# Block-wise attention with a gated feed-forward layer: the transposes of q and k moved from the tensor engine to the DMA crossbar

## The chip, the cores and the metric

The kernel runs on one core of one Trainium2 chip. The metric is the time of one execution on the device in microseconds (us). The engines are named as in the profile: PE (matmul; PEld is its weight load, which overlaps), DVE (VectorE), ACT (ScalarE), POOL (GpSimd), SP (SyncE). Here POOL issues all loads but one small one, and SP issues all stores and, after the change, the crossbar transposes. Sixteen DMA engines serve both queues.

## The reference

```python
q, k, v: [4, 8, 768, 64] float32;  lam: [8]
for each block of the sequence:                     # a decayed linear attention
    out   = (q_b k_b^T * D) v_b + (q_b * lam_pow) kv_state
    kv_state = lam_block * kv_state + (k_b * rev_pow)^T v_b
x   = out as [3072, 512]
res = (sigmoid(x @ w_gate) * (x @ w_val)) @ w_out   # 512 -> 1536 -> 512
```

The recurrence can be cut into blocks of any length. The kernel takes blocks of 128 positions: six blocks, n = 0 to 5, each with all 4 batches and 8 heads.

## The kernel before

q, k and v arrive with positions on the partitions. The scores need q and k with the head dimension on the partitions, so both are transposed. Before the change PE does it: 16 transposes of q and k for each pair of batches ("piece t"), then DVE multiplies q by its decay (QS), and ACT copies k out of PSUM (KS).

```python
qkv = ctx.enter_context(tc.tile_pool(name="qkv", bufs=NSTEP))      # six blocks resident
ps_at ... bufs=5 (PSUM);  ps_ff ... bufs=3 (PSUM)

def piece_t(n, bp):                                  # bp: pair of batches
    tq, tk = two PSUM tiles [128, 2, HP, C] bf16
    ... 8 x nc.tensor.transpose(tq[...], Q[n][...], ident)
    QS[n, bp] = trsb.tile([128, 2, HP, C], BF16, tag="QS", name="QS")
    nc.vector.tensor_tensor(out=QS[n, bp], in0=tq, in1=lamq..., op=ALU.mult)
    ... 8 x nc.tensor.transpose(tk[...], K[n][...], ident)
    KS[n, bp] = trsb.tile([128, 2, HP, C], BF16, tag="KS", name="KS")
    nc.scalar.copy(KS[n, bp], tk)

def piece_s(n, bs): ...   # scores sp <- KS, QS on PE;  piece_m: MT <- sp * mask on DVE
def piece_a(n, bs): ...   # op <- QS, Sb (state) and MT, V on PE; XT <- op on ACT
def make_kd(n): ...       # kd <- K[n] * decay on POOL, for the state update piece_c
def piece_gv(n, ft): ...  # gp = WG x, vp = WV x (4 matmuls each), sg = sigmoid(gp) on ACT,
                          # ht = sg * vp on DVE: one "gate/value unit"; 12 of them a block
def piece_po(n, tt): ...  # po = ht WO (12 matmuls), ob on ACT, store on SP; 4 a block

# the order in which POOL issues loads around block 1:
make_kd(0)
load(1, "qk", 0, 2); load_gv(5, DFF // 6); load(1, "qk", 2, 4)   # halves: batches 0-1, 2-3
load(1, "v", 0, 2);  load(1, "v", 2, 4)
for i in range(3): load_wo(i, NFT // 3)                          # output weights WO
make_kd(1)
...
for i, u in enumerate(units):      # units: gate/value and output units of all blocks in order
    if i in loads:                 # i = start of block n-1
        n = loads[i]
        load(n, "qkv", 0, B)
        make_kd(n)
    u()
    for p in after[i]: p()         # attention pieces of the next block, between the units
```

The attention of block n is spread between the feed-forward units of block n-1. The program's order is fixed on each engine; an engine that waits holds back all that stands behind it.

Of the kernel before, what the change touches and what calls it, by code (L numbers as in the profile page):

```python
# [9 lines left out]
BF16 = mybir.dt.bfloat16  # L10
AF = mybir.ActivationFunctionType
ALU = mybir.AluOpType
# [4 lines left out]
def kernel(  # L17
# [11 lines left out]
    nc = tc.nc  # L29

    B, H, S, D = q.shape
    C = 128
    NSTEP = S // C
    HP = H // 2
# [5 lines left out]
    NB2 = B // 2  # L40

    const = ctx.enter_context(tc.tile_pool(name="const", bufs=1))
    qkv = ctx.enter_context(tc.tile_pool(name="qkv", bufs=NSTEP))
    kdp = ctx.enter_context(tc.tile_pool(name="kdp", bufs=2))
    trsb = ctx.enter_context(tc.tile_pool(name="trsb", bufs=3))
    mtp = ctx.enter_context(tc.tile_pool(name="mtp", bufs=4))
# [19 lines left out]
    wv_r = moe_w_val.rearrange("(mt p) f -> p mt f", p=128)  # L66
    wo_r = moe_w_out.rearrange("(ft p) m -> p ft m", p=128)

    Q, K, V = [], [], []

    for n in range(NSTEP):
        for t, lst in (("qb", Q), ("kb", K), ("vb", V)):
            lst.append(qkv.tile([128, B, H, D], BF16, tag=t, name=t))

    def load(n, what, b0, b1):
        sl = slice(n * C, (n + 1) * C)
        for c in what:
            t, src = {"q": (Q[n], q), "k": (K[n], k), "v": (V[n], v)}[c]
            nc.gpsimd.dma_start(  # L79
                out=t[:, b0:b1],  # L80
                in_=src[b0:b1, :, sl, :].rearrange("b h s d -> s (b h) d"))
# [15 lines left out]
    tri = const.tile([128, C], FP32, tag="tri")  # L97

    load(0, "q", 0, 2)
    for i, base in enumerate((-1, C - 1)):  # L100
        nc.gpsimd.iota(jn[:, i:i + 1], pattern=[[0, 1]], base=base, channel_multiplier=-1,
                       allow_small_or_imprecise_dtypes=True)
    load(0, "k", 0, 2)
    make_upper_triangular(nc, tri, val=1.0, diag=True)
    load(0, "q", 2, 4)
    nc.gpsimd.iota(ip1, pattern=[[1, C]], base=1, channel_multiplier=0,
                   allow_small_or_imprecise_dtypes=True)
# [16 lines left out]
    lamq = const.tile([128, HP, C], BF16, tag="lamq")  # L124
# [11 lines left out]

    QS, KS, MT, XT, KD = {}, {}, {}, {}, {}

    def piece_t(n, bp):
        tq = ps_at.tile([128, 2, HP, C], BF16, name="tq", tag="ps")  # L140
        tk = ps_at.tile([128, 2, HP, C], BF16, name="tk", tag="ps")
        for i in range(2):
            for hp in range(HP):
                nc.tensor.transpose(tq[:, i, hp, :], Q[n][:, 2 * bp + i, 2 * hp:2 * hp + 2, :], ident)  # L144
        QS[n, bp] = trsb.tile([128, 2, HP, C], BF16, tag="QS", name="QS")
        nc.vector.tensor_tensor(out=QS[n, bp], in0=tq,  # L146
                                in1=lamq.unsqueeze(1).to_broadcast([128, 2, HP, C]), op=ALU.mult)
        for i in range(2):
            for hp in range(HP):
                nc.tensor.transpose(tk[:, i, hp, :], K[n][:, 2 * bp + i, 2 * hp:2 * hp + 2, :], ident)  # L150
        KS[n, bp] = trsb.tile([128, 2, HP, C], BF16, tag="KS", name="KS")
        nc.scalar.copy(KS[n, bp], tk)  # L152
# [41 lines left out]
    def make_kd(n):  # L194
        KD[n] = kdp.tile([128, B, H, D], BF16, tag="kd", name="kd")
        nc.gpsimd.tensor_tensor(  # L196
            out=KD[n], in0=K[n],
            in1=kds.unsqueeze(1).unsqueeze(3).to_broadcast([128, B, H, D]), op=ALU.mult)
# [61 lines left out]


    piece_t(0, 0)
    piece_s(0, [0])
    piece_m(0, 0)
    piece_s(0, [1])
    piece_m(0, 1)
    piece_t(0, 1)
    piece_s(0, [2])
    piece_m(0, 2)
# [18 lines left out]
    def place(n, c, t, s, a):  # L288


        for bp in range(2):
            bs = [2 * bp, 2 * bp + 1]
            after[c[bp]].append(lambda bs=bs: piece_c(n - 1, bs))
            after[t[bp]].append(lambda bp=bp: piece_t(n, bp))
            after[s[bp]].append(lambda bs=bs: piece_s(n, bs))
            after[s[bp]].append(lambda b=bs[0]: piece_m(n, b))
            after[s[bp] + (0 if s[bp] == NFT - 1 else 1)].append(lambda b=bs[1]: piece_m(n, b))
        for bp in range(2):
            bs = [2 * bp, 2 * bp + 1]
            after[a[bp]].append(lambda bs=bs: piece_a(n, bs))  # L300
# [4 lines left out]
        place(n, (u0, u0 + 1), (u0 + 2, u0 + 3), (u0 + 4, u0 + 7), (u0 + 8, u0 + 11))  # L305
    loads = {start[n - 1]: n for n in range(2, NSTEP)}
    for i, u in enumerate(units):
        if i in loads:
            n = loads[i]
            load(n, "qkv", 0, B)  # L310
            make_kd(n)
        u()
        for p in after[i]:
            p()
# [30 lines left out]
```

## Time and profile before

| | before |
|---|---|
| median of 3 runs | 247.66 us (247.08 to 247.76) |
| span of the profiled run | 245.1 us |
| PE busy | 226.0 us (92%) |
| a 12 + 4 unit block in the steady part | 37.3 us |

These are lines of the page of the kernel before: the busy time of the engines, then tenths of busy time in 40 slices (9 is 90% or more), then the chain of waits that ended last by engine.

```profile
PE 226.0 (92%) x1572; PEld 117.8 (48%) x1600; DVE 105.3 (43%) x181; ACT 86.3 (35%) x144; POOL 84.7 (35%) x72
...
PE   0578999889999999999999999999999999999993
...
DMA  8999999999299299909943100002200002200022
...
PE 90%; DMA 2%; ACT 2%; issue 2%; DVE 1%; POOL 0%; POOLq 0%; DVEq 0%
```

PE is the limit from about 20 us on. The DMA engines are full in the first 60 us, mostly full until about 120 us, and nearly idle after 140 us.

The timeline of PE around block 1's first transposes and scores follows (start in us, duration in us, engine, line, what, count).

```profile
37.31 0.61 PE L144 MATMUL tq<-ident,qb 128*128 128x128 bf16 x8
37.75 0.61 PE L150 MATMUL tk<-ident,kb 128*128 128x128 bf16 x8
38.20 1.03 PE L228 MATMUL gp<-XT,WG 128*128 128x512 bf16 x3
...
40.02 0.23 PE L164 MATMUL sp_515<-QS,KS 64*128 64x128 bf16 x1
...
50.27 1.02 PE L228 MATMUL gp<-XT,WG 128*128 128x512 bf16 x3 [0.94 <-ACT XT L192]
```

From start to start, sixteen transposes cost 0.89 us (38.20 - 37.31). The groups of instructions on the page give the mean of one transpose as 234 ns, which is its latency; they overlap, so one costs 56 ns of PE time. Anyone who multiplies 160 transposes by 234 ns gets 37 us, four times too much.

The stretches view gives the busy time of each engine in a steady block.

```profile
core 0: us, PE busy (x) PEld busy (x) DVE busy (x) ACT busy (x) POOL busy (x), PEclk, DMA share, GB/s
98.10:135.40 37.30, 36.93 (x269) 19.34 (x272) 17.36 (x30) 13.49 (x22) 12.67 (x8) 1.00 0.99 92
```

### The profile page before, as it was taken

The numbers are of one execution on the slowest core, as the hardware profiler recorded it, in microseconds if no ns is written. First come the engines' busy times: TensorE is split into PE (matmuls) and PEld (weight loads), VectorE is DVE, ScalarE is ACT, GpSimd is POOL, SyncE is SP. The second block draws the span as 40 slices with busy tenths as digits, with TensorE's granted clock in tenths as the row PEclk, the third lists the DMA queues.
The fourth block names the chain that finished last, engine by engine and source line by source line (L and its number), as shares of the span: only waits on it lengthen the run. The fifth ranks groups of instructions, "written<-read, shape, count | busy, mean of one in ns | idle before, by whom it ended". The sixth has DMA issues, their size and how long they took to land.

```text
span 245.1 us, 3880 instructions
## 1 busy us (share of the span) xinstructions
PE 226.0 (92%) x1572; PEld 117.8 (48%) x1600; DVE 105.3 (43%) x181; ACT 86.3 (35%) x144; POOL 84.7 (35%) x72
## 2 busy tenths in 40 slices
PE   0578999889999999999999999999999999999993
PEld 0463545544554554564554564554554554444441
DVE  3481755822637510667510567620467720234300
ACT  3642234442243431342431352432252332333221
POOL 8969945805951980298000190000000000000000
PEclk9999999999999999999999999999999999999999
DMA  8999999999299299909943100002200002200022
GB/s 54 144 181 196 179 174 175 201 157 90 86 146 182 18 76 181 173 3 88 156 15 117 54 4 0 0 3 86 86 3 0 4 0 86 86 3 0 0 86 86
DMA packets 85649, 20.69 MB, mean 84 GB/s; under 512 B 74880, under 2 KB 82560, under 8 KB 85632
## 3 DMA queue, kind: packets, MB, share of 16 engines
q0 software_dynamic: 82032, 14.16, 76.6%
q1 hardware_dynamic: 3600, 6.30, 7.1%
q8 instruction: 12, 0.20, 0.3%
q14 instruction: 5, 0.04, 0.1%
HBM read 28.32 MB, written 6.29 MB: 141 GB/s over the span
## 4 chain that ended last, share of the span: by engine, by line
PE 90%; DMA 2%; ACT 2%; issue 2%; DVE 1%; POOL 0%; POOLq 0%; DVEq 0%
PE vp L234 26%; PE gp L228 26%; PE po L242 25%; PE tk L150 3%; DMA kb<-in_k_dram 2%; PE op L185 2%; PE tq L144 2%; PE cp L204 2%; PE op L178 2%; DVE MT L172 1%; ACT KS L152 1%; ACT XT L192 1%; PE sp_210 L164 0%; PE sp_258 L164 0%; ACT ob L245 0%
## 5 line engine op out<-in xcount | busy, mean ns | idle before, releaser
L237 DVE TENSOR_TENSOR ht<-sg,vp 128x512 bf16<-128x512 bf16 x72 | 49.5, 688 | 109.5 <-PE vp L234 107.6
L228 PE MATMUL gp<-XT,WG 128*128 128x512 bf16 x272 | 72.3, 382 | 2.8 <-ACT XT L192 1.6
L234 PE MATMUL vp<-XT,WV 128*128 128x512 bf16 x283 | 74.1, 381 | 0.5
L231 ACT ACTIVATE sg<-gp 128x512 bf16<-128x512 f32 x72 | 43.1, 598 | 74.3 <-PE gp L228 67.1
L242 PE MATMUL po<-WO,ht 128*128 128x512 bf16 x281 | 63.3, 379 | 0.4
L234 PEld LDWEIGHTS <-WV 128*128 128x128 bf16 x288 | 28.4, 99 | 34.6 <-issue 1.1
L242 PEld LDWEIGHTS <-ht 128*128 128x128 bf16 x288 | 27.7, 98 | 32.7
L196 POOL TENSOR_TENSOR kd<-kb,kds 128x2048 bf16<-128x2048 bf16 x6 | 21.7, 3617 | 58.0 <-PE cp L204 36.0
L228 PEld LDWEIGHTS <-WG 128*128 128x128 bf16 x288 | 26.5, 98 | 30.0 <-issue 2.6
L245 ACT COPY ob<-po 128x512 f32<-128x512 f32 x24 | 14.1, 586 | 49.6 <-PE po L242 49.6
L192 ACT CAST XT<-op 128x512 bf16<-128x512 f32 x24 | 13.0, 588 | 13.8 <-PE op L185 13.8
L152 ACT COPY KS<-tk 128x1024 bf16<-128x1024 bf16 x12 | 12.1, 1012 | 13.6 <-PE tk L150 13.6
L209 POOL TENSOR_TENSOR sd<-Sb,dec 128x512 f32<-128x512 bf16 x16 | 16.1, 1033 | 0.0
L217 DVE TENSOR_TENSOR Sb<-cp,sd 64x256 bf16<-64x256 f32 x32 | 13.5, 421 | 5.4 <-POOL sd L209 4.3
L144 PE MATMUL tq<-ident,qb 128*128 128x128 bf16 x96 | 8.2, 234 | 6.3 <-DMA qb<-in_q_dram 6.3
L79 POOL DMA_DIRECT2D qb<-in_q_dram x8 | 11.9, 1490 | 0.1
L79 POOL DMA_DIRECT2D kb<-in_k_dram x8 | 11.5, 1439 | 0.0
L79 POOL DMA_DIRECT2D vb<-in_v_dram x8 | 11.4, 1437 | 0.0
L144 PEld LDWEIGHTS <-qb 128*128 128x128 bf16 x96 | 6.8, 105 | 8.9 <-DMA qb<-in_q_dram 6.3
L150 PE MATMUL tk<-ident,kb 128*128 128x128 bf16 x96 | 8.2, 235 | 1.6 <-DMA kb<-in_k_dram 1.6
L146 DVE TENSOR_TENSOR QS<-tq,lamq 128x1024 bf16<-128x1024 bf16 x12 | 8.2, 685 | 3.0 <-PE tq L144 2.8
L164 PEld LDWEIGHTS <-KS 64*128 64x128 bf16 x192 | 6.0, 100 | 7.2 <-issue 3.1
(127 smaller groups left out, 123.7 us busy)
## 6 DMA issues: line engine op xcount, KB each, us to landing
out_dram<-ob SPq DMA_DIRECT2D x24, 256.0 KB, 2.0
qb<-in_q_dram POOLq DMA_DIRECT2D x4, 512.0 KB, 8.5
kb<-in_k_dram POOLq DMA_DIRECT2D x4, 512.0 KB, 10.6
vb<-in_v_dram POOLq DMA_DIRECT2D x4, 512.0 KB, 13.0
WG<-in_moe_w_gate_dram POOLq DMA_DIRECT2D x6, 256.0 KB, 9.7
WV<-in_moe_w_val_dram POOLq DMA_DIRECT2D x6, 256.0 KB, 9.9
WO<-in_moe_w_out_dram POOLq DMA_DIRECT2D x3, 512.0 KB, 14.3
qb<-in_q_dram POOLq DMA_DIRECT2D x4, 256.0 KB, 7.2
```

What stands on the lines that cost most here:

```text
L79: nc.gpsimd.dma_start(out=t[:, b0:b1], in_=src[b0:b1, :, sl, :].rearrange("b h s d -> s (b h) d"))
L144: nc.tensor.transpose(tq[:, i, hp, :], Q[n][:, 2 * bp + i, 2 * hp:2 * hp + 2, :], ident)
L150: nc.tensor.transpose(tk[:, i, hp, :], K[n][:, 2 * bp + i, 2 * hp:2 * hp + 2, :], ident)
L152: nc.scalar.copy(KS[n, bp], tk)
L192: nc.scalar.copy(XT[n][:, :, b, :], OP[n, b])
L196: nc.gpsimd.tensor_tensor(out=KD[n], in0=K[n], in1=kds.unsqueeze(1).unsqueeze(3).to_broadcast([128, B, H, D]), op=ALU.mult)
L209: nc.gpsimd.tensor_tensor(out=sd, in0=Sb[:, b], in1=dec.unsqueeze(2).to_broadcast([128, HP, 128]), op=ALU.mult)
L228: nc.tensor.matmul(gp, lhsT=WG[:, mt, fs], rhs=x[:, mt, :], start=(mt == 0), stop=(mt == NMT - 1))
L231: nc.scalar.activation(sg, gp, AF.Sigmoid)
L234: nc.tensor.matmul(vp, lhsT=WV[:, mt, fs], rhs=x[:, mt, :], start=(mt == 0), stop=(mt == NMT - 1))
L237: nc.vector.tensor_mul(HT[n, ft], sg, vp)
L242: nc.tensor.matmul(po, lhsT=HT[n, ft][:, tt * 128:(tt + 1) * 128], rhs=WO[:, ft, :], start=(ft == 0), stop=(ft == NFT - 1))
```

## The change: intent and diff

The intent is to take work off the engine that limits. A DMA can transpose on its way from SBUF to SBUF, through a crossbar, so k needs neither PE nor PSUM nor an ACT copy, and q reaches DVE without PE. Block 0 stays with PE, since nothing can hide its latency. The four new tiles (QR and KR, two each) take room, so four blocks of q, k, v are kept instead of six.

```diff
-    qkv = ctx.enter_context(tc.tile_pool(name="qkv", bufs=NSTEP))
+    qkv = ctx.enter_context(tc.tile_pool(name="qkv", bufs=4))
 ...                       (tiles of q, k, v are now made at their load)
+    def transpose_by_dma(n):
+        QR[n] = trsb.tile([128, B, HP, C], BF16, tag="QR", name="QR", bufs=2)
+        kt = trsb.tile([128, B, HP, C], BF16, tag="KR", name="KR", bufs=2)
+        for dst, src in ((QR[n], Q[n]), (kt, K[n])):
+            nc.sync.dma_start_transpose(out=dst.rearrange("p b g c -> p (b g) c"),
+                                        in_=src.rearrange("p b h d -> p (b h d)"))
+        for bp in range(2):
+            KS[n, bp] = kt[:, 2 * bp:2 * bp + 2]
+
     def piece_t(n, bp):
+        if n > 0:
+            QS[n, bp] = trsb.tile([128, 2, HP, C], BF16, tag="QS", name="QS")
+            nc.vector.tensor_tensor(out=QS[n, bp], in0=QR[n][:, 2 * bp:2 * bp + 2],
+                                    in1=lamq..., op=ALU.mult)
+            return
 ...
     for i, u in enumerate(units):
+        if i == 6:
+            transpose_by_dma(1)
         if i in loads:
             n = loads[i]
             load(n, "qkv", 0, B)
             make_kd(n)
+            transpose_by_dma(n)
```

More of the change, by code (lines that the diff above doesn't have):

```diff
@@ L67 @@
     wo_r = moe_w_out.rearrange("(ft p) m -> p ft m", p=128)
-    Q, K, V = [], [], []
-    for n in range(NSTEP):
-        for t, lst in (("qb", Q), ("kb", K), ("vb", V)):
-            lst.append(qkv.tile([128, B, H, D], BF16, tag=t, name=t))
+    Q, K, V = {}, {}, {}
     def load(n, what, b0, b1):
@@ L77, in load @@
         for c in what:
-            t, src = {"q": (Q[n], q), "k": (K[n], k), "v": (V[n], v)}[c]
+            lst, src = {"q": (Q, q), "k": (K, k), "v": (V, v)}[c]
+            if n not in lst:
+                lst[n] = qkv.tile([128, B, H, D], BF16, tag=c + "b", name=c + "b")
+            t = lst[n]
             nc.gpsimd.dma_start(
@@ L137 @@
     QS, KS, MT, XT, KD = {}, {}, {}, {}, {}
-    def piece_t(n, bp):
+    QR = {}
+    def transpose_by_dma(n):
[6 more added lines that the diff above has]
+            KS[n, bp] = kt[:, 2 * bp:2 * bp + 2]
+    def piece_t(n, bp):
+        if n > 0:
+            QS[n, bp] = trsb.tile([128, 2, HP, C], BF16, tag="QS", name="QS")
+            nc.vector.tensor_tensor(out=QS[n, bp], in0=QR[n][:, 2 * bp:2 * bp + 2],
+                                    in1=lamq.unsqueeze(1).to_broadcast([128, 2, HP, C]), op=ALU.mult)
+            return
         tq = ps_at.tile([128, 2, HP, C], BF16, name="tq", tag="ps")
```

## The prediction

> **What bounds the kernel.** PE. The page gives PE 226.0 of 245.1 us (92%), DVE, ACT and POOL under 45%; the chain of waits is 90% PE. By the stretches, each 37.3 us block from 98 us on has PE busy 36.9 us. Only PE time, or a new PE wait, counts.
>
> **Removed.** 160 PE transposes (blocks 1 to 5) and ten KS copies on ACT. A transpose's mean of 234 ns overstates it: they overlap. In the PE timeline a piece (16 transposes) runs from 37.31 to 38.20 and from 65.84 to 66.73 us: 0.89 us. Ten pieces give 8.9 us, all on the chain: the ceiling is 238.8 us. The ACT copies (1.01 us each) are off the chain. QS stays on DVE, reading SBUF instead of PSUM.
>
> **Added.** Ten crossbar transposes of 512 KB on the SP queue, with no duration in this trace. The Trainium skill ("DMA: Bandwidth & Descriptors", "Latency and other measured facts") states 261 GB/s measured for a DMA transpose; my estimate from it is 2 us of data plus about 2 us until landing (a 256 KB store lands in 2.0 us here): 4 us for q, 6 us for the pair, on idle queues.
>
> **Blocks 2 to 5.** By the instruction order a block's transposes stand on SP behind the stores of the block before the last, so they start about 1 us into a block. DVE needs Q after the third gate/value unit (6.3 us in), the scores need K after the fifth (about 9.6 us). A pair of 6 us fits; block 2 has more time. I expect no wait and 4 x 1.78 = 7.1 us saved. Four resident blocks cost nothing: blocks 4 and 5 load long after blocks 0 and 1 are finished with.
>
> **Block 1 pays.** PE could start on the first half of the batches; the crossbar waits for whole tiles. From issue plus landing time, the second half of q lands at 37.4 us, of k at 39.3 us, while the scores ran at 40.0 us (39.1 without transposes). The DMA engines are 90% busy then. The same page ("Queues, rings and completion order") has them take queues in turn by packet, so I halve the rate: k transposed lands at 45 to 47 us. DVE stands in QS, PE before block 1's first scores, 6 to 8 us. Less the 1.78 us saved there this is +4 to +6 us, and up to 1.5 us for a PE slow after the gap (16 op matmuls took 1.1 us at 16.8 us, after waits, 0.64 us at 47 us).
>
> **Sum.** 247.66 - 7.1 + 5.3 + 1.5 = about 247.4 us. I predict 247.5 us, range 242.5 to 259. Faster by over 2%: 0.13; within 2%: 0.62; slower by over 2%: 0.25.
>
> **What would show it.** PE transposes 32 instead of 192, KS copies 2. Block period from 98 us on 35.5 instead of 37.3 us. The longest new PE wait: block 1's scores on the DMA of KR, 6 to 8 us, with DVE QS waiting for QR. Transposes landing in 4 to 6 us idle, 6 to 9 in block 1. Later blocks: no wait on QR or KR over 0.5 us.
>
> **What would make it wrong.** The transposes' speed. Over about 4 us each on idle engines, the pair misses the 9.6 us deadline, and blocks 3 to 5 lose their gain and more: 260 us and beyond. If block 1's pair lands by 43 us, the result is 242 to 243 us. Slower loads beside the transposes would delay the output weights or block 2; I expect that hidden.

## The result, and the profile after

The changed kernel takes 262.92 us (median of 4 runs, 261.96 to 265.55) against 247.68 us before (4 runs). The ratio is 1.064, with a 95% interval from 1.056 to 1.072: slower by 6.4%. The predicted range ended at 259 us.

The same lines of the page after, with the row of the clock that PE was granted (in tenths of full speed):

```profile
PE 222.4 (85%) x1440; PEld 109.4 (42%) x1440; DVE 110.3 (42%) x181; ACT 77.0 (30%) x134; POOL 87.8 (34%) x72
...
PE   0559991008789999999999999999999999999994
...
PEclk9986999555999999999999999999999999999999
DMA  8999999999999729927479829000273001300022
...
PE 73%; DMA 17%; POOL 5%; DVE 1%; issue 1%; ACT 1%; POOLq 0%; DVEq 0%
```

There is one hole in the PE row, at the seventh to ninth slice (39 to 59 us), inside the stretch where the DMA engines are full. The timeline of PE shows it:

```profile
39.27 1.03 PE L249 MATMUL vp<-XT,WV 128*128 128x512 bf16 x4
59.81 0.29 PE L179 MATMUL sp_487<-QS,KR 64*128 64x128 bf16 x1 [19.51 <-DMA KR<-kb]
...
60.77 1.89 PE L243 MATMUL gp<-XT,WG 128*128 128x512 bf16 x4
62.45 1.91 PE L249 MATMUL vp<-XT,WV 128*128 128x512 bf16 x4
64.16 1.76 PE L243 MATMUL gp<-XT,WG 128*128 128x512 bf16 x4
65.75 1.03 PE L249 MATMUL vp<-XT,WV 128*128 128x512 bf16 x4
...
72.56 1.02 PE L243 MATMUL gp<-XT,WG 128*128 128x512 bf16 x4 [0.94 <-ACT XT L207]
```

PE has nothing to do from 40.3 to 59.8 us, 19.5 us (the expectations below say 19.7). Afterwards groups of four matmuls start about 1.7 us apart instead of 0.86: the clock has fallen to half (the row of fives). The first unit that needs block 1's attention starts at 72.56 instead of 50.27 us, 22.3 us late. The view of waits names what PE and DVE waited for (us in total, times, longest):

```profile
PEld L179 <- DMA KR<-kb: 20.4, 2, 20.0
...
PE sp_487 L179 <- DMA KR<-kb: 19.5, 1, 19.5
DVE QS L152 <- DMA QR<-qb: 14.4, 1, 14.4
```

The SP timeline shows how long each transpose held the issuing sequencer. Block 1 is shown first, then block 3.

```profile
37.41 8.15 SPq L144 DMA_TRANSPOSE QR<-qb  x1
45.66 7.93 SPq L144 DMA_TRANSPOSE KR<-kb  x1
...
119.70 2.16 SPq L144 DMA_TRANSPOSE QR<-qb  x1
121.96 3.39 SPq L144 DMA_TRANSPOSE KR<-kb  x1
```

From issue to landing, block 1's pair took 16.3 and 14.1 us (KR lands at 45.7 + 14.1 = 59.8 us), block 3's 5.4 and 4.9 us. The fastest, in block 5, took 4.6 us each. The steady blocks are what the change was made for (stretches view, columns as before):

```profile
120.40:155.90 35.50, 35.50 (x243) 17.53 (x241) 18.07 (x30) 11.65 (x20) 13.56 (x8) 1.00 0.99 104
```

A block takes 35.5 us in place of 37.3, and PE is busy throughout. So the account closes: block 1 costs +22.3 us, blocks 2 to 5 give 4 x 1.78 = 7.1 us, together +15.2; the spans differ by 260.2 - 245.1 = 15.1 us. The whole question is why block 1's transposes took 16 and 14 us.

### The profile page after: what moved, and what is told of

It reads as the page before. It is cut to its first block, busy times and chain, and to the rows that moved or that the text cites. A ratio compares the mean times of both kernels' runs of the same rounds, so it can differ in the third digit from the quotient of the medians.

```text
span 260.2 us, 3598 instructions
## 1 busy us (share of the span) xinstructions
PE 222.4 (85%) x1440; PEld 109.4 (42%) x1440; DVE 110.3 (42%) x181; ACT 77.0 (30%) x134; POOL 87.8 (34%) x72
## 4 chain that ended last, share of the span: by engine, by line
PE 73%; DMA 17%; POOL 5%; DVE 1%; issue 1%; ACT 1%; POOLq 0%; DVEq 0%
PE po L257 24%; PE gp L243 21%; PE vp L249 21%; DMA KR<-kb 5%; DMA WO<-in_moe_w_out_dram 5%; DMA kb<-in_k_dram 3%; DMA WV<-in_moe_w_val_dram 3%; PE op L200 2%; PE op L193 2%; POOL kd L211 1%; PE cp L219 1%; POOL qb L78 1%; POOL vb L78 1%; POOL kb L78 1%; DVE MT L187 1%
## 5 line engine op out<-in xcount | busy, mean ns | idle before, releaser
L243 PE MATMUL gp<-XT,WG 128*128 128x512 bf16 x288 | 77.4, 393 | 1.6 <-ACT XT L207 1.6
L249 PE MATMUL vp<-XT,WV 128*128 128x512 bf16 x288 | 75.8, 387 | 0.0
L243 PEld LDWEIGHTS <-WG 128*128 128x128 bf16 x288 | 27.4, 100 | 33.7 <-issue 5.2
L224 POOL TENSOR_TENSOR sd<-Sb,dec 128x512 f32<-128x512 bf16 x16 | 19.2, 1229 | 0.0
L152 DVE TENSOR_TENSOR QS<-QR,lamq 128x1024 bf16<-128x1024 bf16 x10 | 12.2, 1227 | 14.5 <-DMA QR<-qb 14.4
L179 PE MATMUL sp_487<-QS,KR 64*128 64x128 bf16 x4 | 0.6, 306 | 19.5 <-DMA KR<-kb 19.5
L179 PEld LDWEIGHTS <-KR 64*128 64x128 bf16 x160 | 4.8, 98 | 25.2 <-DMA KR<-kb 20.4
L200 PE MATMUL op<-MT,vb 128*64 128x128 bf16 x192 | 8.4, 225 | 0.8 <-DVE MT L187 0.6
L159 PE MATMUL tq<-ident,qb 128*128 128x128 bf16 x16 | 2.1, 311 | 6.5 <-DMA qb<-in_q_dram 6.5
L200 PEld LDWEIGHTS <-vb 128*64 128x64 bf16 x192 | 6.2, 111 | 2.4 <-issue 1.1
## 6 DMA issues: line engine op xcount, KB each, us to landing
WO<-in_moe_w_out_dram POOLq DMA_DIRECT2D x3, 512.0 KB, 15.7
```

The costliest lines, as they stand in the source:

```text
L200: nc.tensor.matmul(OP[n, b][us, hp, :], lhsT=V[n][:, b, 2 * hp + u, :], rhs=MT[n, b][:, u, hp, :], start=(n == 0 and hp == 0), stop=(hp == ...
L224: nc.gpsimd.tensor_tensor(out=sd, in0=Sb[:, b], in1=dec.unsqueeze(2).to_broadcast([128, HP, 128]), op=ALU.mult)
L243: nc.tensor.matmul(gp, lhsT=WG[:, mt, fs], rhs=x[:, mt, :], start=(mt == 0), stop=(mt == NMT - 1))
L249: nc.tensor.matmul(vp, lhsT=WV[:, mt, fs], rhs=x[:, mt, :], start=(mt == 0), stop=(mt == NMT - 1))
```

## The experiments

Theory L: the loads that POOL has queued at that time (v of block 1, the output weights, block 2) keep the crossbar transposes from getting turns on the DMA engines. Rivals: S, the first crossbar transposes of a program are slow by themselves; Q, the issuing sequencer sets the pace; H, an even share of the engines, as the prediction had it, with something else behind the rest.

### PE keeps block 1 as well

```diff
-        if n > 0:
+        if n > 1:
             QS[n, bp] = ...
-        if i == 6:
-            transpose_by_dma(1)
```

> Blocks 0 and 1 transposed by PE, blocks 2 to 5 by the crossbar. Theory L (the loads queued in block 1 starve the crossbar; the later blocks gain as predicted): the 22 us of block 1 vanish, four blocks save 1.78 us each, 247.7 - 7.1 = 240.5 us (239.5 to 242), scores never wait for KR over 0.5 us. Rival S (the first crossbar transposes of a program are slow whatever runs beside them): block 2's pair would then be the first and land 16 and 14 us after issue, as block 1's did, and PE would stall before the scores of block 2: 245 us or more.

Measured: 241.80 us median of 4 runs (241.16 to 242.21), before 247.14; ratio 0.978 (0.976 to 0.981), faster beyond the noise by about 2%. The result is correct. The 22 us are gone, so they belonged to block 1. Block 2's pair, now the first of the program, landed in 10.0 and 5.5 us and made PE wait for nothing; rival S expected 16 and 14. But one new wait appeared, of 2.3 us, in block 3, where I had expected none over 0.5. Its SP timeline there:

```profile
97.46 5.24 SPq L144 DMA_TRANSPOSE QR<-qb  x1
102.79 3.27 SPq L144 DMA_TRANSPOSE KR<-kb  x1
```

Its PE timeline:

```profile
108.23 0.62 PE L179 MATMUL sp<-QS,KR 64*128 64x128 bf16 x16 [2.32 <-DMA KR<-kb]
```

And its POOL timeline, the last load of block 4:

```profile
89.54 1.70 POOL L78 DMA_DIRECT2D vb<-in_v_dram  x1
```

This load was issued at 89.5 us, and by the DMA records the load queue was moving pieces at full rate until about 101.5 us. Block 3's q transpose, issued at 97.5, was held 5.2 us, and its first piece moved at 101.8 us; block 4's, with no loads beside it, was held 2.1 us. That looks like theory L again, on a small scale; a later run tests it.

### The loads of block 2 held back

A read of one column of KR on POOL, ahead of the loads, makes them wait without removing any wait that is needed.

```diff
+    def hold_pool_until_kr1():
+        scr = const.tile([128, 1], BF16, tag="scr", name="scr")
+        nc.gpsimd.tensor_copy(scr, KS[1, 0][:, 0, 0, 0:1])
 ...
             n = loads[i]
+            if n == 2:
+                hold_pool_until_kr1()
             load(n, "qkv", 0, B)
```

> The changed kernel, but GpSimd reads one column of block 1's KR before it issues the loads of block 2, so these start only after KR has landed; v of block 1 and the output weights still run beside the transposes. Theory L: the engines are free of loads once the output weights are in (about 48 us), so KR lands at 49 to 53 us instead of 59.8 and the wait of PE before the first scores falls from 19.7 to 9 to 13 us. Rival S, and rival Q (the sequencer that issues the transposes sets the pace): KR lands at 59 to 60 us as before.

Measured: one run, correct, 256.96 us. In this run and the other single ones I read the landings and waits, which are far larger than any noise here, and not the total. From the view of waits:

```profile
PE sp L183 <- DMA KR<-kb: 15.7, 1, 15.7
```

KR landed at 46.0 + 9.4 = 55.4 us and PE waited 15.7 us: earlier than 59.8, but later than my 49 to 53. The direction is theory L's, the size is not. The loads still beside it (v of block 1 and the output weights) weighed more than I had given them; the last of them ended between 49 and 53 us by the DMA records. Rivals S and Q expected no movement.

### All other loads held back

```diff
     load(1, "qk", 2, 4)
+    transpose_by_dma(1)
+    hold_pool_until_kr1()
     load(1, "v", 0, 2)
     ...
-        if i == 6:
-            transpose_by_dma(1)
```

> As the one before, but v of block 1, the output weights and block 2 are all held back until KR has landed, so nothing runs beside the crossbar once q and k of block 1 are in. Theory L: q issues at about 37 us and lands within 5 us, KR lands at 42 to 45 us, PE waits 3 to 5 us before the first scores; afterwards it waits for v and the output weights, which come late, so the total is not the point. Rivals S and Q: QR still takes 16 us, KR 14 us, KR lands near 60 us.

Measured: one run, correct, 251.1 us. The SP timeline of this kernel:

```profile
37.39 2.10 SPq L144 DMA_TRANSPOSE QR<-qb  x1
39.59 2.45 SPq L144 DMA_TRANSPOSE KR<-kb  x1
```

Its PE timeline:

```profile
44.32 0.62 PE L183 MATMUL sp<-QS,KR 64*128 64x128 bf16 x16 [4.00 <-DMA KR<-kb]
44.88 1.59 PE L247 MATMUL gp<-XT,WG 128*128 128x512 bf16 x4
```

The same two transposes, at the same place, issued at the same 37.4 us, land in 4.6 and 4.7 us instead of 16.3 and 14.1. They are still the first of the program and still issued by SP, so S and Q fall. The wait of PE is 4.0 us instead of 19.5: 15.5 us of it was the loads (3.8 us those of block 2, by the run before; 11.7 us v of block 1 and the output weights), and 4.0 us is what is left because whole tiles arrive late and the pair needs 6.9 us (37.4 to 44.3). One part of the expectation failed: the profile shows no wait of PE for v or for the output weights. The total stayed above the kernel before for other reasons that the trace shows: PE waited 3.5 us at the second scores for a QS that took 3.53 us beside kd on POOL (see the last two runs), and its clock was at half from 45.2 to 48.6 and from 55.5 to 62.3 us.

### Four buffers alone

```diff
-    qkv = ctx.enter_context(tc.tile_pool(name="qkv", bufs=NSTEP))
+    qkv = ctx.enter_context(tc.tile_pool(name="qkv", bufs=4))
 ...   (the kernel before, tiles of q, k, v made at their load)
```

> The kernel before with four resident blocks of q, k, v in place of six, transposes all on PE. Both theories: the loads of blocks 4 and 5 find buffers long free, so 247.7 us within 0.3%. If four buffers cost something, it shows as a GpSimd wait before the loads of blocks 4 and 5, and more than 1 us.

Measured: 247.51 us, before 247.14; ratio 1.001 (0.998 to 1.004). This part of the change costs nothing.

### The loads put behind the transposes

The kernel with PE for block 1, and POOL waits for KR of block n-1 before it loads block n.

```diff
+            if n > 2:
+                hold_pool_until_kr(n - 1)     # reads one column of KS[n - 1, 0] on POOL
             load(n, "qkv", 0, B)
```

> PE for blocks 0 and 1, crossbar for 2 to 5, and GpSimd issues the loads of block n only after KR of block n-1 has landed (n = 3, 4, 5). In the run with PE for block 1, block 3's q transpose was held 5.2 us beside the tail of block 4's loads, and PE waited 2.3 us for KR. Theory L: with those loads behind it the pair of block 3 takes as long as that of block 4 (held 2.1 and 2.2 us, landing in 4.6 and 4.7 us), the wait goes, and the time falls by about 2.3 us to 239 to 240 us. Rival (the 2.3 us had another cause, such as the stores on the same queue): no change from 241.8 us.

Measured: 240.51 us median of 5 runs (240.15 to 240.94), before 247.57; ratio 0.973 (0.971 to 0.976). Correct. It is the fastest version. The SP timeline for block 3:

```profile
97.70 2.05 SPq L144 DMA_TRANSPOSE QR<-qb  x1
99.84 2.28 SPq L144 DMA_TRANSPOSE KR<-kb  x1
```

The hold is 2.05 us, the pair lands in 4.6 and 4.7 us, and no wait of PE or DVE for KR or QR is left in the profile. The time is just above the 239 to 240 us that I expected.

> The kernel of the first run again, beside the two others on one chip, for a comparison in the same rounds: 241.8 us, 2 us above the kernel whose loads come after the transposes.

The kernel without the held loads, in the same rounds: 242.25 us, ratio 0.979 (0.976 to 0.982). So putting the loads behind the transposes is worth 1.4 us by the means and 1.7 us by the medians, where I expected 2.3; every run with the loads behind (240.15 to 240.94) was faster than every run without (241.09 to 242.61).

### Loads added beside a block that had none

```diff
+    def beside_block4(ob):
+        scr = const.tile([128, 1], FP32, tag="scrb", name="scrb")
+        nc.gpsimd.tensor_copy(scr, ob[:, 0:1])        # sets the moment
+        for i, src in enumerate((q, k)):
+            dummy = const.tile([128, B, H, D], BF16, tag=f"dummy{i}", name=f"dummy{i}")
+            nc.gpsimd.dma_start(out=dummy, in_=src[:, :, 0:C, :].rearrange("b h s d -> s (b h) d"))
 ...
+        if i == 50:
+            beside_block4(OB[2, 2])
```

> The run before with two loads added that nobody needs: 512 KB each, in the 128-byte pieces of q and k, issued just before the transposes of block 4, which otherwise run alone. Theory L (the crossbar's queue gets few turns until the queued loads are through): 8192 pieces of 32 ns on 16 engines are 16 us of load, so block 4's KR lands at 149 to 156 us instead of about 142, and PE waits 6 to 12 us before block 4's first scores, though neither block 1 nor a late q or k is in it. Rival H (an even share of the engines' time, as I had predicted): q's transpose is held about 4 us in place of 2, KR lands by 146 us, and PE waits 2 us or less. Rival S (first transposes are slow): no wait at all.

The rest of the kernel is that of "The loads put behind the transposes". Measured: one run, correct, 248.20 us, 7.7 us above the version without the added loads. The SP timeline:

```profile
132.78 5.51 SPq L144 DMA_TRANSPOSE QR<-qb  x1
138.46 5.77 SPq L144 DMA_TRANSPOSE KR<-kb  x1
```

The PE timeline, at block 4's first scores:

```profile
147.30 1.03 PE L183 MATMUL sp<-QS,KR 64*128 64x128 bf16 x16 [6.08 <-DMA KR<-kb]
```

q landed in 11.8 us (4.6 without the loads), k in 8.8 us (4.7), and PE waited 6.1 us where it had not waited at all. KR landed at 147.3 us, a little under my 149 to 156 (the first added load was issued 2.7 us before the transposes), and above rival H's 146 with a wait of at most 2 us. Rival S is excluded here too. Loads beside the transposes are enough to slow them, in a block that has nothing else in common with block 1.

The DMA records of the traces show what an even share misses. One transpose of 512 KB is about 2080 pieces of mostly 256 bytes (the SP queue has 20,800 more pieces than before, for ten transposes). Counted by the microsecond, there are two states:

- Nothing of the transpose moves yet. In this last run, from 133.0 to 135.5 us, the load queue moved 2393 pieces and the transposes none; the first piece of q moved 4.4 us after its issue. In the changed kernel block 1's q also took 4.4 us to its first piece, and with no loads beside it (block 3 with the loads put behind) 1.3 us.
- Both queues move, and then in equal numbers. In the changed kernel it was about 155 pieces of each per us from 43 to 49 us, where the loads were the output weights in pieces of 1024 bytes (about 96 ns each; one of a transpose 31 ns), and about 410 of each from 52 to 56 us, where the loads came in pieces of 128 bytes. Alone, the transposes move about 800 per us.

So half the rate, as predicted, holds beside the short pieces, and a fifth of it beside the long ones. Block 1's q took 10.8 us from its first piece to its last (2.6 alone), and k 5.5 us (2.5 alone). This is read from the records; no run here changed the length of the pieces alone. Why the first piece waits is not settled either. That the queued loads delay the transposes is.

### PE kept busy during the wait, twice

The slow clock after the gap was the second term of the prediction (1.5 us). To take it away, matmuls that nobody reads were put before block 1's first scores in the changed kernel.

```diff
     def piece_s(n, bs):
+        if n == 1 and bs[0] == 0:
+            warm = ps_at.tile([128, HP, C], FP32, name="warm", tag="ps")
+            for i in range(80):                      # 94 in the second run
+                nc.tensor.matmul(warm..., lhsT=WG[:, 0, 0:128], rhs=WV[:, 0, 0:512],
+                                 start=True, stop=True)
```

> The changed kernel with 80 matmuls of 512 columns, whose result nobody reads, put before block 1's first scores: at 216 ns each they fill 17.3 us of the 19.7 us that PE waits for KR. If the clock of PE drops because it idled, and drops at a cost of 2.4 us in the gate/value matmuls after the wait plus 0.3 us in the scores, this kernel is 2 to 3 us faster than the changed one, 260 to 261 us, its gate/value matmuls after the wait take 0.86 us for four, and the granted clock is 0.99 or more. If the low clock has another cause, or costs nothing, the time stays at 263 us. Transposes and loads are not touched: KR should land near 60 us either way.

Measured: 263.22 us, before 247.56; ratio 1.066 (1.061 to 1.070). No gain. It did not test its question: 3.4 us of idle time were left before the scores, and the clock fell all the same.

> As the run before with 94 matmuls in place of 80. That run left PE idle for 3.4 us before the scores and the clock fell all the same, so it did not test what it was meant to. 94 matmuls at 216 ns end at about 60 us, when KR lands, and leave a gap under 1 us. If the low clock follows from the idle time and costs what it shows: four gate/value matmuls after the wait take 0.86 us, granted clock 0.99 or more over 60 to 66 us, total 2 to 3 us under the changed kernel's 262.9 us. If the clock is as expected but the time stays near 263 us, the slow matmuls lay in the shadow of another wait (block 1's second QS on DVE).

Measured: 263.64 us, before 246.99; ratio 1.066 (1.061 to 1.071). The PE timeline of this run:

```profile
60.15 0.62 PE L183 MATMUL sp<-QS,KR 64*128 64x128 bf16 x16 [0.64 <-DMA KR<-kb]
...
62.44 1.03 PE L247 MATMUL gp<-XT,WG 128*128 128x512 bf16 x4
63.30 1.03 PE L253 MATMUL vp<-XT,WV 128*128 128x512 bf16 x4
68.60 1.03 PE L183 MATMUL sp<-QS,KR 64*128 64x128 bf16 x16 [4.27 <-DVE QS L152]
...
74.30 1.02 PE L247 MATMUL gp<-XT,WG 128*128 128x512 bf16 x3 [0.74 <-ACT XT L211]
```

Its DVE timeline, block 1's second QS:

```profile
64.51 4.03 DVE L152 TENSOR_TENSOR QS<-QR,lamq 128x1024 bf16<-128x1024 bf16 x1
```

Its POOL timeline at the same time:

```profile
64.38 3.61 POOL L215 TENSOR_TENSOR kd<-kb,kds 128x2048 bf16<-128x2048 bf16 x1 [16.40 <-PE vp L253]
```

Now the clock stayed up after the wait for KR (the groups of four matmuls start 0.86 us apart, and the granted clock is 1.00 from 60 to 66 us), yet the time did not fall. PE ran into another wait: block 1's second QS, which took 4.03 us on DVE instead of 0.69, because POOL had just begun kd of block 2. In the changed kernel this QS ended at 68.0 us, 0.55 us after kd, and the second scores began at 68.1: up to there the slow matmuls had been in the shadow of QS, and the second branch of the expectation holds. The run does not show what a clock that never falls would give: the 4.27 us wait brought it down again (half from 67.0 to 73.8 us), and from the second scores to the first dependent unit it took 5.7 us (68.60 to 74.30), against 4.5 in the changed kernel.

In the changed kernel QS takes 0.68 to 0.69 us where POOL is idle, and it took always 0.68 to 0.69 us before the change, when its first input was in PSUM. "SBUF — State Buffer" of the Trainium skill, section "SBUF: two separate sides", says that a DVE instruction with two inputs in SBUF and a POOL instruction that reads SBUF exclude each other for their whole length. Here QS began 0.13 us after kd and ended 0.55 us after it, which agrees; in the changed kernel and in the first of these two runs it also ended 0.55 us after kd, having taken 1.73 and 2.30 us, while block 3 to 5's QS, with POOL idle in the fastest version, took 0.68. The cost is new with the change and was not in the prediction.

## Why the prediction was wrong, point by point

- The size of the saving was right. Sixteen transposes cost 0.89 us; the steady block fell from 37.3 to 35.5 us as predicted; blocks 2 to 5 gave 7.1 us.
- The speed of an undisturbed transpose was right: 4.6 us from issue to landing for q, and 6.8 us for the pair (97.70 to 104.5 us with the loads behind it), predicted 4 and 6.
- The place of the loss was right: block 1's scores on KR, with DVE in QS.
- The step that failed is "so I halve the rate: k transposed lands at 45 to 47 us". KR landed at 59.8 us, and PE waited 19.5 us in place of 6 to 8. The Trainium skill's page "DMA: Bandwidth & Descriptors", section "Queues, rings and completion order", on which the step drew, says that an engine drains a whole packet from one queue, typically 9 to 17 descriptors, before it goes to the next. That is not half of the time for each queue when one queue's turns are longer; I read a fair share into it. With the loads taken away the landing fell to 4.6 and 4.7 us; with loads added to block 4 it rose to 11.8 and 8.8 us. By the DMA records two things stood in place of my half: the first piece of q moved 4.4 us after issue (1.3 alone), and beside the long pieces of the output weights the transposes moved at a fifth of their rate, so that q took 10.8 us (2.6 alone). Only k, beside short pieces, moved at about half. The loads were there throughout: their queue went on moving pieces until about 70 us.
- The term for the slow PE (1.5 us) was mis-sized and misplaced. Three groups of four matmuls lost 2.4 us, but with that loss taken away the second scores began no earlier, because the second QS on DVE, slowed by POOL, was waited for there anyway. From the first scores to the first dependent unit the changed kernel took 12.7 us, the kernel before 10.3.
- "Slower loads beside the transposes would delay ... block 2; I expect that hidden": not quite. kd of block 2 waited 15.9 us for k (9.8 before), began at 63.9 us, and so fell on block 1's second QS.
- In the sum: +5.3 and +1.5 for block 1 should have been +22.3.

## What to carry to other kernels

Work moved from a busy engine to the DMA engines is free only where their queues are short: before you count the gain, list what else is queued at that time, and in pieces of what length, and do not count on half the rate. Here the first piece waited 4.4 us, and after that the two queues moved equal numbers of pieces, so that long pieces cost the transposes most. To count on the transfer coming after all of the loads would have been too much: in the changed kernel KR landed at 59.8 us, and the loads ended at about 70. A transfer that something waits for soon should be issued ahead of bulk loads, and loads that nobody needs soon can be made to wait for it (here a one-column read on the issuing engine, worth 1.4 to 1.7 us). Keep the old way for the stages in which the new path is crowded: PE for the first two blocks and the crossbar for the other four, with the loads behind, gave 240.5 us, where the crossbar for five gave 262.9 and PE for all 247.6.

## What the Trainium skill lacked or had wrong

- "DMA: Bandwidth & Descriptors", "Rules for kernel authors", says that a transpose next to ordinary DMAs needs nothing. It stands there against corruption, and for that every run here agrees: the results are correct. Of time it says nothing: 4.6 us alone, 16.3 us beside queued loads. No page gives a figure for a crossbar transpose beside loads issued by GpSimd.
- The same page, "Queues, rings and completion order": turns by whole packets. The counts here agree with turns (155 pieces of each queue per us beside 1024-byte pieces, 410 of each beside 128-byte ones), but cannot show how long a turn is. The page does not say how many pieces of a transpose make a packet, and it has nothing on the 4.4 us to the first piece beside loads (1.3 us without).
- The same page, "Latency and other measured facts": 261 GB/s for a DMA transpose, measured on one kernel. Here it was less: block 3's pair with the loads put behind moved its 4096 pieces of 256 bytes in 5.1 us (99.0 to 104.1 by the DMA records), from which I estimate 206 GB/s.
- "TensorE: Matmul & The Clock Gate", "Part 4: PE-mode transpose", gives about 275 ns for a 128x128 transpose in a kernel. As a latency that is near the 234 ns here; the cost in a row is 56 ns, which that section does not give and which decides what removing transposes is worth.
- The same page, "Why this matters for your kernels": no PE gaps over about 3 us. The runs agree: the clock held over gaps of 2.3 and 2.5 us, and fell to half in or after gaps of 3.4, 3.5, 4.0, 4.3, 6.1, 15.7 and 19.5 us. At the start, where PE works in short bursts, it also fell without such a gap (at 17.8 us in the changed kernel, with no gap over 1.2 us in the 8 us before).
- "SBUF — State Buffer", "SBUF: two separate sides": the exclusion of DVE and POOL. The runs agree: 0.69 us alone, 4.03 us beside a POOL multiply of 3.61 us. It lacks nothing here; moving one input from PSUM to SBUF brought an instruction under that rule.
